# First block of a light convolution with a ReGLU layer: who fetches taps and x, and the order of the first convolution's matmuls

## The chip, the cores and the metric

The kernel runs on one core of a Trainium2 chip. The metric is the device time of one execution in microseconds (us), as the median of several runs. A core has TensorE (PE, matrix products into PSUM; its weight loads are listed apart as PEld), VectorE (DVE), ScalarE (ACT), GpSimd (POOL) and SyncE (SP). SP, ACT and POOL can issue DMA transfers. Each engine works through its own list of instructions in order and waits for the others by semaphores.

## The reference

Eight sequences x of 4096 tokens with 192 channels go through a causal convolution of 7 taps. The taps are a softmax over each of the 8 heads' 7 weights, and a head covers 24 channels. The result goes through a gated layer: 1536 gate columns with ReLU, times 1536 value columns, times an output matrix back to 192 channels.

```python
w = weight - np.max(weight, axis=-1, keepdims=True)
w = np.exp(w)
w = w / (np.sum(w, axis=-1, keepdims=True) + 1e-09)
x_pad = np.concatenate([np.zeros((B, pad, D), dtype=np.float32), x], axis=1)
x_unf = x_pad[:, idx, :].reshape(B, S, K, H, group)
out = np.einsum('hk,bskhg->bshg', w, x_unf)
...
gate = np.maximum(x @ w_gate, 0.0)
val = x @ w_val
return (gate * val @ w_out).astype(np.float32)
```

## The kernel before

Two sequences, called the streams (st), are worked on at a time, one on each half of the 128 partitions. A unit is 1024 tokens of both streams, and 16 units cover everything. The 192 channels are cut into three pieces of 64 (c), so a piece of both streams fills 128 partitions.

For most units the convolution is done off TensorE: x is turned by DMA transposes and multiplied with the taps on VectorE, ScalarE and GpSimd while TensorE does the gate, value and output products of the unit before. The first unit has no unit before it. Its convolution is done on TensorE, as products with band matrices, in two blocks of 512 tokens (`first_block` and `second_block`). The change lies in the first block and in what leads up to it.

What leads up to it, with the lines of the kernel before:

- SyncE fetches the 8 x 7 weights into `wr` (L110), then the body of stream 0's first 512 tokens in fp32 into the room `prods` (L131). GpSimd fetches the body of stream 1, cast to fp16, into `x_h` (L134), then the first 96 tokens of both streams (L135), then pieces of the gate and value matrices Wg and Wv (L170).
- VectorE sets `ones`, and ScalarE takes the Exp of it into `spare`, which nobody reads (L141 to L144). An Exp needs a table, and the load of the table stands right ahead of the first Exp on ScalarE's list.
- TensorE multiplies constants (`warm_up`, L154) while it has no data.
- The softmax: VectorE finds the maximum (L272), ScalarE takes the exponential (L275), VectorE sums, inverts and multiplies (L277 to L281).
- The bands: TensorE spreads the softmax over 112 rows (L289), VectorE puts it on diagonals (L299), 14 matmuls put the diagonals in their places (L309), and VectorE casts the bands to fp16 in four pieces (L336): heads 0 to 2, head 3, heads 4 and 5, heads 6 and 7.
- ScalarE casts stream 0's body from the room into `x_h` (L321), in two parts.

Then `conv_dense` makes the first block. The 512 tokens are cut into five steps (jj): the first 96 tokens are step 0, and four steps of 104 tokens follow. For each piece c it walks over the steps 1, 2, 3, 4, 0; in each over two halves (`second`, for the two heads that a run of 32 channels can touch), the two streams and two runs of 32 channels (k2). One such matmul has up to 32 output columns of the array, and `tile_position` (0, p0) with p0 = 64 st + 32 k2 says which of the four groups of 32 columns it uses. A piece needs 40 matmuls (five steps, two halves, two streams, two runs), the block 120. The pieces are finished one after the other, and each is copied out of PSUM into `xc` as soon as it is done: pieces 0 and 1 by ScalarE, piece 2 by VectorE (L388).

`gate_val` then makes the gate and value products (L550), 128 columns at a time. Its first tile takes the pieces in the order 0, 1, 2. Its second tile needs the copy of the next columns of Wg to the other partition half, which VectorE makes behind its copy of piece 2 (L177 from L805).

The kernel is scheduled by hand: the order of the statements is the order on each engine, and the tile framework adds the semaphore waits.

Of the kernel before, what the change touches and what calls it, by code (L numbers as in the profile page):

```python
# [8 lines left out]
FP = mybir.dt.float32  # L9
# [3 lines left out]
ACTF = mybir.ActivationFunctionType  # L13
# [4 lines left out]
def kernel(  # L18
# [12 lines left out]
    nc = tc.nc  # L31

    B, S, D = x.shape
    H, KW = weight.shape
# [29 lines left out]
    const = ctx.enter_context(tc.tile_pool(name="const", bufs=1))  # L64
# [9 lines left out]
    psum = ctx.enter_context(tc.tile_pool(name="psum", bufs=4, space=bass.MemoryType.PSUM))  # L74
# [32 lines left out]
    SEG = 16  # L107
    NSEG = SUB // SEG
    wr = const.tile([H, KW], FP)
    nc.sync.dma_start(out=wr[:], in_=weight)  # L110
    room = apool.tile([128, KW, NCH, LPOOL], FP, name="prods")

    def stage(p0, rows, st, n_st, jj, n):
        at = room[p0 : p0 + rows, 0, 0, 0:1]
        dims = [[D * GSUB, n_st], [D, n], [1, D]]
        return bass.AP(
            tensor=at.tensor,
            offset=at.offset + D * (GSUB * st + jj),
            ap=[at.ap[0]] + [d for d in dims if d[1] > 1],
        )  # L120
# [3 lines left out]
    def body(st):  # L124
# [7 lines left out]
    steps = const.tile([SUB, 64], I32)  # L132
# [3 lines left out]
        out=xts[0][PAD : PAD + FIRST, 0, :, :],  # L136
        in_=bass.AP(
            tensor=x.tensor, offset=x.offset, ap=[[D, FIRST], [NB * S * D, 2], [1, D]]
        ),
    )  # L140
    ones = const.tile([H, 1], FP)  # L141
    nc.vector.memset(ones[:], 1.0)
    spare = const.tile([H, 1], FP)
    nc.scalar.activation(spare[:], ones[:], ACTF.Exp)  # L144
    nc.vector.memset(xts[0][0:PAD, 0, :, :], 0.0)

    places = const.tile([SUB, 2 * SUB], F16)
# [27 lines left out]
    def both_halves(copy, s, dst):  # L175
        cols = slice(CUTS[s], CUTS[s + 1])
        copy(out=dst[64:128, :, cols], in_=dst[0:64, :, cols])  # L177
# [82 lines left out]
    with nc.allow_low_precision("zero and one"):  # L260
        nc.vector.tensor_tensor(
            out=same[:], in0=col[:, 0:SEG], in1=s_of[:].to_broadcast([SUB, SEG]), op=ALU.is_equal
        )
        nc.vector.tensor_scalar(
            out=places[:, SUB - SEG : SUB - SEG + NROW],
# [7 lines left out]
        out=mx[:], in_=wr[:], axis=mybir.AxisListType.X, op=ALU.max, negate=True  # L273
# [6 lines left out]
    with nc.allow_low_precision("rounded as the band is"):  # L280
        nc.vector.tensor_scalar(  # L281
            out=soft[:],
# [7 lines left out]
        out=spread[0:SUB, 0, 0:H],  # L290
# [7 lines left out]
    with nc.allow_low_precision("products with one and zero"):  # L298
        nc.vector.tensor_tensor(  # L299
            out=diag[:],  # L300
# [6 lines left out]
    for a in range(2):  # L307
        for b in range(NSEG):
            nc.tensor.matmul(  # L309
                out=(bps, spread)[a][:, a, HB * SEG * b : HB * SEG * (b + 1)],  # L310
# [9 lines left out]
    for cols in (slice(0, 64), slice(64, D)):  # L320
        nc.scalar.copy(  # L321
            out=xts[0][0:ROWS0, 1:GSUB, 0, cols],
            in_=stage(0, ROWS0, 0, 1, 1, GSUB - 1)[:, :, cols],
# [22 lines left out]
    def band(h):  # L346
        return bands[h]
# [2 lines left out]

    def conv_dense(g, c, ps, bank):


        xt = xts[g]
        toks = GROUPS[g][1]
        t0 = toks[0]
        ends = toks[1:] + [t0 + WIN]
        for jj in (1, 2, 3, 4, 0):  # L360
            col, n = toks[jj] - t0, ends[jj] - toks[jj]
            rows = n + PAD
            for second in range(2):
                for st in range(2):
                    for k2 in range(2):
                        k = 2 * c + k2
                        h0, h1 = 32 * k // G, (32 * k + 31) // G
                        h, m = (h0, G * h1 - 32 * k) if second else (h1, 32)
                        p0 = 64 * st + 32 * k2
                        nc.tensor.matmul(  # L370
                            out=ps[p0 : p0 + m, bank, col : col + n],
                            lhsT=xt[0:rows, jj, st, 32 * k : 32 * k + m],
                            rhs=band(h)[0:rows, 0:n],
                            start=True,
                            stop=True,
                            tile_position=(0, p0),
                            skip_group_check=True,
                        )

    def first_block():  # L380
        xc[0] = xcpool.tile([128, NCH, UNIT], F16, name="xc")
        both_halves(nc.vector.tensor_copy, 0, Wg)
        both_halves(nc.vector.tensor_copy, 0, Wv)
        for c in range(NCH):
            ps = psum.tile([128, 2, 512], FP, name="ps")
            conv_dense(0, c, ps, 0)
            copy = nc.vector.tensor_copy if c == 2 else nc.scalar.copy
            copy(out=xc[0][:, c, 0:WIN], in_=ps[:, 0, :])  # L388

    def second_block():  # L390
        two, one = [psum.tile([128, 2, 512], FP, name="ps") for _ in range(2)]
        conv_dense(1, 0, two, 0)
        conv_dense(1, 1, two, 1)
        nc.scalar.copy(out=xc[0][:, 0:2, WIN : 2 * WIN], in_=two[:])
        conv_dense(1, 2, one, 0)
        nc.vector.tensor_copy(out=xc[0][:, 2, WIN : 2 * WIN], in_=one[:, 0, :])
# [392 lines left out]


    first_block()
    taps = const.tile([H, KW], FP)
    nc.scalar.activation(taps[:], ex[:, 0:KW], ACTF.Copy, scale=sm[:])
    tap = const.tile([128, NCH, KW], FP)
    for h in range(H):
        r = G * h
        while r < G * (h + 1):
            c, n = r // 64, min(64 - r % 64, G * (h + 1) - r)
            nc.sync.dma_start(
                out=tap[r % 64 : r % 64 + n, c, :],  # L800
                in_=taps[h : h + 1, :].unsqueeze(1).to_broadcast([1, n, KW]),
# [98 lines left out]
```

## Time and profile before

| what | us |
|---|---|
| median of 3 runs | 762.16 |
| the runs | 761.86, 762.16, 766.11 |
| span of the profiled execution, first to last instruction | 759.9 |
| TensorE busy in it | 756.1 |
| VectorE busy | 707.4 |
| ScalarE busy | 617.3 |
| GpSimd busy | 404.9 |

The profile is of one execution. Its span covers the instructions; the runs' time has 2.26 us around it that no instruction shows. Times in rows are counted from the span's start. In the chain of waits each row is a start, a length and the work that the end was waiting for at that time. In the timeline a row is a start, a length, the engine, the line, the operation, out<-in with shapes, the count of merged instructions, and in brackets the idle time before it with what ended it.

### The profile page before, as it was taken

Reading aid. Unit: us, or ns where it says so; the run is one execution under the profiler, and the core shown is the slowest. Engines: PE = TensorE matmul, PEld = TensorE weight load, DVE = VectorE, ACT = ScalarE, POOL = GpSimd, SP = SyncE. Lnnn points to the kernel's source line nnn. Section 1 sums busy time; section 2 is a strip of 40 time slices with the busy share of each in tenths; the row PEclk is TensorE's granted clock in tenths of the full one; section 3 lists DMA queues with packets and bytes.
Section 4 is the critical chain, followed back from the end, with each engine's and each line's share of the span. In section 5 each row is a group of like instructions: output and inputs, shape, how many; then the busy total and the mean of one; then the engine's idle time right before and its main releaser. Section 6 shows DMA issues by size and latency. Waiting matters only on the chain.

```text
span 759.9 us, 30608 instructions
## 1 busy us (share of the span) xinstructions
PE 756.1 (99%) x13623; PEld 484.0 (64%) x13623; DVE 707.4 (93%) x768; ACT 617.3 (81%) x719; POOL 404.9 (53%) x263
## 2 busy tenths in 40 slices
PE   9999999999999999999999999999999999999998
PEld 5495555555666666666666666666666776666548
DVE  7998999999999999999999999999999999999891
ACT  6887887978879798897988879788798887976671
POOL 9519449094580936819276291863908548091000
PEclk9999999999999999999999999999999999999999
DMA  9969029688395894949759498594957939654732
GB/s 118 132 113 136 16 68 157 162 107 181 94 184 146 91 180 105 190 128 105 195 93 184 119 138 180 81 186 114 170 145 100 189 98 160 140 107 113 185 87 85
DMA packets 231308, 100.33 MB, mean 132 GB/s; under 512 B 185288, under 2 KB 220424, under 8 KB 231176
## 3 DMA queue, kind: packets, MB, share of 16 engines
q1 hardware_dynamic: 189928, 82.71, 53.1%
q0 software_dynamic: 41104, 15.57, 20.7%
q8 instruction: 106, 1.74, 1.0%
q14 instruction: 26, 0.21, 0.1%
q10 hardware_dynamic: 144, 0.10, 0.0%
HBM read 31.48 MB, written 47.19 MB: 104 GB/s over the span
## 4 chain that ended last, share of the span: by engine, by line
PE 99%; ACT 0%; issue 0%
PE ps L550 66%; PE ps L658 29%; PE ps L579 3%; PE ps L628 1%; PE ps L154 0%; PE ps L370 0%; PE ps L309 0%; PE ps L411 0%; ACT acc L605 0%; PE ps L289 0%
## 5 line engine op out<-in xcount | busy, mean ns | idle before, releaser
L562 DVE TENSOR_TENSOR hT<-gr,ps 128x1024 f16<-128x1024 f16 (+1 forms) x386 | 469.0, 1216 | 30.0 <-ACT gr L561 3.3
L561 ACT ACTIVATE gr<-ps 128x1024 f16<-128x1024 f32 (+1 forms) x386 | 393.3, 1020 | 100.7 <-PE ps L550 100.3
L498 POOL TENSOR_TENSOR prods<-prods 128x1344 f32<-128x1344 f32 x70 | 212.9, 3042 | 268.7 <-DVE prods L494 265.3
L550 PE MATMUL ps<-xc,Wg 64*64 64x512 f16 (+1 forms) x4320 | 321.9, 376 | 0.0
L550 PE MATMUL ps<-xc,Wv 64*64 64x512 f16 (+1 forms) x4320 | 321.6, 376 | 0.0
L658 PE MATMUL ps<-hT,Wo 64*64 64x512 f16 x4032 | 220.3, 376 | 0.0
L550 PEld LDWEIGHTS <-Wg 64*64 64x64 f16 (+1 forms) x4320 | 154.0, 106 | 94.9 <-issue 0.7
L550 PEld LDWEIGHTS <-Wv 64*64 64x64 f16 (+1 forms) x4320 | 152.7, 105 | 95.8 <-issue 0.3
L658 PEld LDWEIGHTS <-Wo 64*64 64x64 f16 x4032 | 140.2, 107 | 77.4
L522 DVE SCALAR_TENSOR_TENSOR acc<-x_r,tap,acc 128x576 f32<-128x576 f16 x225 | 165.3, 814 | 0.0
L492 ACT ACTIVATE prods<-x_r,tap 128x448 f32<-128x448 f16 x222 | 127.2, 659 | 0.0
L680 ACT COPY x_h<-ps 128x2048 uint16<-128x2048 uint16 x28 | 51.8, 1848 | 8.8 <-PE ps L658 8.8
L208 POOL DMA_DIRECT2D x_e<-in_x_dram x58 | 46.9, 818 | 12.3 <-ACT acc L508 12.0
L472 POOL COPY x_p<-x_e 128x960 f16<-128x960 f16 (+1 forms) x58 | 50.5, 912 | 0.5 <-DMA x_e<-in_x_dram 0.5
L498 POOL TENSOR_TENSOR xc<-prods 128x1344 f16<-128x1344 f32 x14 | 42.5, 3037 | 1.1
L680 POOL COPY y<-x_h 128x2048 uint16<-128x2048 uint16 x14 | 26.6, 1897 | 23.3 <-ACT x_h L736 23.3
L522 DVE SCALAR_TENSOR_TENSOR xc<-x_r,tap,acc 128x576 f16<-128x576 f16 x45 | 34.1, 813 | 0.0
L508 ACT ACTIVATE acc<-x_r,tap 128x576 f32<-128x576 f16 x45 | 31.4, 765 | 0.0
L494 DVE TENSOR_SCALAR prods<-x_r,tap 128x448 f32<-128x448 f16 x70 | 27.7, 448 | 0.0
L579 PE MATMUL ps<-Wo,hT 64*128 64x192 f16 x576 | 24.6, 243 | 0.0
L579 PEld LDWEIGHTS <-hT 64*128 64x128 f16 x576 | 23.9, 94 | 0.5
L736 ACT COPY x_h<-ps 128x512 f32<-128x512 f32 x14 | 8.2, 587 | 10.9 <-ACT x_h L680 5.5
(62 smaller groups left out, 91.6 us busy)
## 6 DMA issues: line engine op xcount, KB each, us to landing
out_dram<-out_s SPq DMA_DIRECT2D x62, 384.0 KB
held<-x_h SPq DMA_DIRECT2D x14, 512.0 KB
held<-x_h SPq DMA_DIRECT2D x28, 256.0 KB
held<-y SPq DMA_DIRECT2D x14, 512.0 KB
x_e<-in_x_dram POOLq DMA_DIRECT2D x34, 192.0 KB, 6.7
x_e<-in_x_dram POOLq DMA_DIRECT2D x24, 240.0 KB, 5.4
x_r<-x_p SPq DMA_TRANSPOSE x131
out_s<-held SPq DMA_TRANSPOSE x56
```

Source lines behind the costliest of these rows:

```text
L208: first = nc.gpsimd.dma_start(out=xe[:, j0 + start : j0 + n, st, :, :].rearrange("p j c r -> p j (c r)"), in_=bass.AP(tensor=x.tensor, off ...
L472: nc.gpsimd.tensor_copy(out=xp[:, j0 : j0 + n, :, st, :], in_=xe[:, j0 : j0 + n, st, :, :])
L492: engine.activation(out=out, in_=in_, func=ACTF.Copy, scale=scale)
L498: nc.gpsimd.tensor_tensor(out=pr[:, 0] if k < KW - 1 else xc[v + 1][:, :, LDVE:UNIT], in0=pr[:, 0], in1=pr[:, k], op=ALU.add,)
L508: nc.scalar.activation(out=accs[v][:, c, :], in_=shifted(v, c, 0, 0), func=ACTF.Copy, scale=tap[:, c, 0:1],)
L522: nc.vector.scalar_tensor_tensor(out=xc[v][:, c, 0:LDVE] if k == KW - 1 else acc[:, c, :], in0=shifted(v, c, k, 0), scalar=tap[:, c, k : k ...
L550: nc.tensor.matmul(out=pss[i][m : m + M, st, :], lhsT=W[64 * st : 64 * st + 64, c, 128 * f + m : 128 * f + m + M], rhs=xcb[64 * st : 64 * ...
L561: nc.scalar.activation(out=gr[:, sts], in_=pss[0][:, sts], func=ACTF.Relu)
L562: nc.vector.tensor_tensor(out=h[:, f, sts], in0=gr[:, sts], in1=pss[1][:, sts], op=ALU.mult)
L579: mm = nc.tensor.matmul(out=outs[q], lhsT=h[64 * r : 64 * r + 64, f, st, 128 * q : 128 * (q + 1)], rhs=Wo[64 * r : 64 * r + 64, f, :], sta ...
L658: mm = nc.tensor.matmul(out=ps[bank][64 * half : 64 * half + 64], lhsT=Wo[64 * r : 64 * r + 64, f, d : d + 64], rhs=hs[w][64 * r : 64 * r ...
L680: copy(out=pt[:], in_=src[:].bitcast(U16).rearrange("p b (t l) -> p b l t", l=2))
```

## The change

Three edits. ScalarE's queue issues the transfer of the weights into `wr`, so that SyncE's first transfer is x. The pair `ones` and `spare` is gone. In `first_block` the steps 1 to 4 of the pieces 0 and 1 go ahead, first all of stream 0, then all of stream 1; step 0 of these pieces follows, and then piece 2 in the old order. `conv_dense` takes the steps and the streams as arguments for it.

```diff
-    nc.sync.dma_start(out=wr[:], in_=weight)
+    nc.scalar.dma_start(out=wr[:], in_=weight)
...
-    ones = const.tile([H, 1], FP)
-    nc.vector.memset(ones[:], 1.0)
-    spare = const.tile([H, 1], FP)
-    nc.scalar.activation(spare[:], ones[:], ACTF.Exp)
...
-    def conv_dense(g, c, ps, bank):
+    def conv_dense(g, c, ps, bank, steps=(1, 2, 3, 4, 0), streams=(0, 1)):
...
-        for jj in (1, 2, 3, 4, 0):
+        for jj in steps:
...
-                for st in range(2):
+                for st in streams:
...
+        pss = [psum.tile([128, 2, 512], FP, name="ps") for _ in range(2)]
+        for st in range(2):
+            for c in range(2):
+                conv_dense(0, c, pss[c], 0, (1, 2, 3, 4), (st,))
         for c in range(NCH):
-            ps = psum.tile([128, 2, 512], FP, name="ps")
-            conv_dense(0, c, ps, 0)
+            if c == 2:
+                pss.append(psum.tile([128, 2, 512], FP, name="ps"))
+            ps = pss[c]
+            conv_dense(0, c, ps, 0, (1, 2, 3, 4, 0) if c == 2 else (0,))
             copy = nc.vector.tensor_copy if c == 2 else nc.scalar.copy
             copy(out=xc[0][:, c, 0:WIN], in_=ps[:, 0, :])
```

How the instructions stand on an engine, with what each waits for, is shown at two places. The first is the start of ScalarE's list, before. DMAHW0 is the transfer of the weights, DMAHW1 the transfer of x by SyncE.

```order
L144 ACT_TABLE_LOAD
L144 ACTIVATE spare<-ones 8x1 [waits DVE_49]
L275 ACTIVATE ex<-wr,mx 8x7 [waits DMAHW0_49,DVE_49]
L321 CAST x_h<-prods 110x4x64 [waits DMAHW1_49]
L321 CAST x_h<-prods 110x4x128
```

The same place now:

```order
L110 DMA wr<-in_weight_dram 8x7
L271 ACT_TABLE_LOAD [waits DMAHW0_49]
L271 ACTIVATE ex<-wr,mx 8x7 [waits DVE_49]
L317 CAST x_h<-prods 110x4x64 [waits DMAHW1_49]
L317 CAST x_h<-prods 110x4x128
```

The table load stood first and waited for nothing. Now it stands behind the issue of the weights' transfer, ahead of the real exponential, and the wait for that transfer stands on the load.

The second place is the start of the first convolution on TensorE, before. band_182 is the tile with the bands of heads 0 to 2, and DMASW0 is GpSimd's transfer of stream 1's body.

```order
L370 LDWEIGHTS x_h [waits Activation_49]
L370 MATMUL ps<-band_182,x_h 32x104 [waits DVE_49]
L370 LDWEIGHTS x_h
L370 MATMUL ps<-band_182,x_h 32x104
L370 LDWEIGHTS x_h [waits DMASW0_49]
L370 MATMUL ps<-band_182,x_h 32x104
```

The same place now, where band_178 is that same tile of heads 0 to 2:

```order
L366 LDWEIGHTS x_h [waits Activation_49]
L366 MATMUL ps<-band_178,x_h 32x104 [waits DVE_49]
L366 LDWEIGHTS x_h
L366 MATMUL ps<-band_178,x_h 32x104
L366 LDWEIGHTS x_h
L366 MATMUL ps<-band_178,x_h 24x104
L366 LDWEIGHTS x_h
L366 MATMUL ps<-band_178,x_h 16x104
```

Before, stream 1 was needed by the third matmul, and four matmuls of a kind in a row went to the four column groups. Now two of a kind go to the two groups of stream 0, then two of the next kind to the same two groups, and stream 1 is first waited for ahead of the 33rd matmul.

## The prediction

> **What bounds the kernel now.** I read the page's head first, then the chain of waits in order of time, then the timeline of the first 16 us, and last single groups and transfers in that stretch.
>
> The page's head says how much room there is at all.
>
> ```profile
> span 759.9 us, 30608 instructions
> PE 756.1 (99%) x13623; PEld 484.0 (64%) x13623; DVE 707.4 (93%) x768; ACT 617.3 (81%) x719; POOL 404.9 (53%) x263
> ```
>
> TensorE is busy for 756.1 of 759.9 us. An edit can only matter by making TensorE wait, by giving it more to do, or by changing the speed at which it does it. The chain (start, length, what) shows where the edited code lies in it.
>
> ```profile
> 0.78 2.72 PE ps L154 x6
> 3.50 0.18 PE ps L289
> 3.68 0.54 PE ps L154
> 4.22 0.75 PE ps L309 x14
> 4.96 0.32 PE ps L154
> 5.28 1.95 PE ps L370 x117
> 7.23 6.74 PE ps L550 x60
> 13.97 1.62 PE ps L370 x113
> 15.59 24.71 PE ps L550 x228
> ...
> 756.88 0.02 issue
> 756.90 0.32 ACT acc L605
> ```
>
> The change touches only what lies before the first gate matmul (L550, 7.23). From 15.59 to the end the chain is matmuls without a gap, so whatever the first gate tiles lose or gain is handed to the end one for one. What the start waits for is in the timeline (start, length, engine, line, in brackets the idle time before it and who ended it):
>
> ```profile
> 0.73 1.28 ACT L144 ACT_TABLE_LOAD   x1 [0.73 <-PEq L884]
> 0.74 0.40 SPq L110 DMA_DIRECT2D wr<-in_weight_dram  x1
> 1.20 0.34 SPq L131 DMA_DIRECT2D prods<-in_x_dram  x1
> 1.41 0.89 POOL L134 DMA_DIRECT2D x_h<-in_x_dram  x1 [0.40 <-issue]
> 2.03 0.20 ACT L144 ACTIVATE spare<-ones 8x1 f32<-8x1 f32 x1
> 2.11 0.15 DVE L272 TENSOR_REDUCE mx<-wr 8x1 f32<-8x7 f32 x1 [0.30 <-DMA wr<-in_weight_dram]
> 2.29 0.30 ACT L275 ACTIVATE ex<-wr,mx 8x7 f32<-8x7 f32 x1
> 2.30 0.69 POOL L135 DMA_DIRECT2D x_h<-in_x_dram  x1
> 3.42 0.16 PEld L289 LDWEIGHTS <-soft 8*112 8x112 f16 x1 [0.84 <-DVE soft L281]
> 3.71 0.29 DVE L299 TENSOR_TENSOR diag<-ps,same 112x128 f16<-112x128 f32 x1 [0.40 <-PE ps L289]
> 4.63 1.28 DVE L336 CAST band<-ps 128x336 f16<-128x336 f32 x4 [0.62 <-PE ps L309]
> 4.65 0.93 ACT L321 CAST x_h<-prods 110x256 f16<-110x256 f32 x2 [2.06 <-DMA prods<-in_x_dram]
> 5.21 2.02 PE L370 MATMUL ps<-band,x_h 110*32 110x104 f16 x120
> 6.34 1.08 ACT L388 CAST xc<-ps 128x512 f16<-128x512 f32 x2 [0.76 <-PE ps L370]
> 7.17 0.39 PE L550 MATMUL ps<-xc,Wg 64*128 64x512 f16 x2
> 7.28 0.69 DVE L388 CAST xc<-ps 128x512 f16<-128x512 f32 x1 [0.37 <-PE ps L370]
> 8.00 0.56 DVE L177 COPY Wg<-Wg 64x768 f16<-64x768 f16 x1
> 8.62 0.33 PEld L550 LDWEIGHTS <-Wg 64*128 64x128 f16 x5 [0.27 <-DVE Wg L177]
> ```
>
> Two chains meet at 5.21. One is the band: taps landed (2.11), exponential (2.29), softmax, spread matmul (3.42), diagonal (3.71), 14 matmuls, band in fp16 (4.63). The other is x: landed and cast by ScalarE (4.65). The groups by form and the transfers (KB, us from issue to landing) show how close they are.
>
> ```profile
> L336 DVE CAST band<-ps 128x336 f16<-128x336 f32 x1 | 0.5, 509 | 0.6 <-PE ps L309 0.6
> L321 ACT CAST x_h<-prods 110x256 f16<-110x256 f32 x1 | 0.4, 405 | 2.1 <-DMA prods<-in_x_dram 2.1
> x_h<-in_x_dram POOLq DMA_DIRECT2D x1, 168.0 KB, 3.8
> x_h<-in_x_dram POOLq DMA_DIRECT2D x1, 72.0 KB, 3.7
> ```
>
> The first band is ready at 4.63 + 0.51 = 5.14, the first cast of x at 4.65 + 0.41 = 5.06, the second stream's body at 1.41 + 3.8 = 5.2, the first rows at 2.30 + 3.7 = 6.0. Three conditions end within 0.15 us of each other, so moving only one of them earlier is worth about 0.1 us. Moving one later costs all of it.
>
> **The table load loses its cover.** The removed pair (ones, and the Exp of ones into spare) did no arithmetic that anybody reads, but ScalarE's table load stood in front of it and waited for nothing: 0.73 to 2.01, beside the flight of the taps, which the reduction sees landed at 2.11. In the changed program the load stands in front of the real exponential and waits for the taps' transfer, as the order of ScalarE shows. It starts at about 2.11, ends at 2.11 + 1.28 = 3.39, and the exponential follows at 3.41 where it stood at 2.29: **+1.12 us** on the band's chain, with nothing beside it. Queued behind the load on ScalarE are the exponential and the two casts of x. The exponential would end at 3.71, x has not landed by then, and the casts lose nothing. Behind the exponential wait VectorE's sum, TensorE's spread and every step down to 5.21, which becomes 6.33.
>
> The trace does not show a taps transfer issued by ScalarE beside x. At best it lands as now (SyncE issued it at 0.74, and ScalarE is free at 0.73). At worst it shares the engines with x and loses what x's issue took beside it, about 0.4 us. I take 0, since the transfer is 0.2 KB, and keep 0.4 for the range.
>
> **x first on SyncE.** x is issued at 0.74 instead of 1.20, so by estimate it lands 0.46 us earlier and the first cast is done near 4.6. The band is ready only at 5.14 + 1.12 = 6.26. Worth **0**. If the load did not wait, it would be worth the 0.1 above.
>
> **The order by streams.** One stream's matmuls fill two of the four 32-column groups (p0 is 64 st + 32 k2). The 64 moved matmuls (two channel pieces, four steps, two halves, two k2, two streams) therefore go in 32 rounds of two where they went in 16 rounds of four. A round lasts as long as one group needs for 104 columns. At full speed the gate matmuls, which fill two groups of 64 rows, give 24.71/228 = 0.108 us each, so 0.217 us for 512 columns in a group: 44 ns for 104. The second block's 120 in 1.62 (13.97) give at most 56 ns for a round of four. I take 50 ns, so 16 more rounds cost **+0.8 us** at full speed. At the start speed the warm-up of 384 columns took 0.32 us (4.96): 87 ns, and 16 rounds are **+1.4 us**. What the order was to hide, the arrivals at 5.2 and 6.0, is over at 6.33 anyway.
>
> It has a second price. Channel piece 0 was complete after 40 matmuls and ScalarE copied it at 6.34, while TensorE was still convolving. Now pieces 0 and 1 are complete only 16 matmuls after the 64, and just piece 2 (40 matmuls) is left to hide two copies of 0.54 us.
>
> **The speed of TensorE.** Its weight loads in the first convolution, in two windows (count: min/median/max ns, first and last start):
>
> ```profile
> L370 PEld LDWEIGHTS <-x_h x24: 90/137/147, 5.2 to 5.6; 110*32 110x32 f16 x12, 110*24 110x24 f16 x6, 110*16 110x16 f16 x6
> L370 PEld LDWEIGHTS <-x_h x88: 82/93/97, 6.0 to 7.0; 110*32 110x32 f16 x32, 110*8 110x8 f16 x16, 102*32 102x32 f16 x12, 110*24 110x24 f16 x8
> ```
>
> TensorE turned to full speed between 5.6 and 6.0, say 5.8, about 5.0 us after its first matmul, and it had worked nearly without a gap since 0.78. In the changed kernel the warm-ups end at 3.50 as now, but the spread comes at 3.42 + 1.12 = 4.54: a hole of 1.0 us that the trace of before does not have. From below the hole costs nothing (full speed still at 5.8). From above the count of 5.0 us begins again at 4.7, when the warm-up behind the spread starts, and full speed comes at 9.7. I take the upper end, since in this trace full speed came only after an unbroken stretch.
>
> The Trainium skill, "TensorE: Matmul & The Clock Gate", section "What's actually happening", says that the clock doubles after a free-running window of about 3.4 us was busy, sustained. The trace agrees with it: 5.0 us lies between one window and two. For the changed kernel the page puts full speed between 8.1 and 11.5, and by my reckoning the time would be an estimated 764.4 to 765.7 us.
>
> **The sum**, on the profile's clock. Convolution from 6.33. One stream at a time, at half speed: 32 x 0.087 = 2.78, to 9.11. First rows of pieces 0 and 1: 4 rounds, 0.34, to 9.45. Piece 2: 3 rounds to 9.7, then 7 x 0.05, to 10.06, and about 0.2 us for the last matmul's own length: 10.26, against 7.23 now. From there to the second gate tile the path is VectorE's, copy of piece 2 and then the copy of Wg: 8.62 - 7.23 = 1.39. So the second gate tile starts at 11.65 instead of 8.62, **+3.0**. The path over ScalarE ends earlier: piece 0 done at 9.28, copied about 0.25 later in 0.54, first gate matmul near 10.2, twelve of 0.108 us, 11.5. From 8.62 to 13.97 stand 48 matmuls, 5.2 us of work in 5.35, so up to 0.15 of small waits can be absorbed; I take 0.1. **Net +2.9 us**: the span goes from 759.9 to 762.8. The median of the runs, 762.16, lies 2.26 us above the span, so the time is 762.16 + 2.9 = **765.1 us** (0.4% more).
>
> **Rivals.**
>
> *Full speed is not delayed (0.36).* The hole is short and the matmuls around it suffice. Then 32 x 0.05 = 1.6 to 7.93, first rows to 8.13, piece 2 to 8.63, end 8.83, second gate tile by VectorE at 10.22. By ScalarE: copy of piece 0 from 8.28 to 8.82, of piece 1 to 9.36, first tile done at about 10.3. That is +1.7, less 0.1: **763.8**. For it: the hole is 1.0 us of 5.8. Against it: the unbroken stretch that the trace needed.
>
> *The load doesn't wait after all (0.05).* If ScalarE starts the load on its own while the taps fly, the convolution starts at 5.21 and full speed comes at 5.8. Seven rounds at half speed, 25 at full, first rows to 7.27, end near 8.0, first tile by ScalarE at about 9.46: +0.8, less 0.1, **762.9**. Against it stands the wait written on the load.
>
> *Not slower (0.04).* The same, and the rounds of two cost no more than rounds of four, because the weight loads and not the columns set the pace. Then 120 matmuls take the second block's 1.62 instead of 1.95, as arrivals no longer hold them, and **761.8** results. It decides if the load starts before about 1.0, so that it ends before the reduction at 2.26. The two-group rate above speaks against the second half.
>
> *The load costs more than its row (0.05).* If the load cannot be followed at once and takes its own length again, 1.28 us more fall on the chain: **766.4**. In the trace the activation started at 2.03, right behind the load's end at 2.01, which speaks against it. The Trainium skill, "ScalarE: Activation LUTs", section "What ACT_TABLE_LOAD costs", gives 1283 ns and a drain of about 1380 ns on top. The trace agrees with the first number and shows no drain, and the measurement decides.
>
> **Chances and range.** Forecast 0.50, full speed in time 0.36, and 0.14 for the others, as given. The range takes in the first two: from 763.8 less 0.6 (full-speed rounds of 44 ns instead of 50, and the 0.3 between the two lower runs, 761.86 and 762.16) = 763.2, to 765.1 plus 0.4 for late taps and 0.6 for half speed to the end of the first tile = 766.1. What falls outside is 0.14. One per cent is 7.6 us, about what a measurement of this kernel can tell from no change, and no case reaches half of that: the same 0.97. Faster by over 1% 0.01, slower by over 1% 0.02, for a mechanism that I don't see.
>
> **What would show it.** In the profile of the changed kernel: the table load begins at about 2.1, not 0.7, and ends right before the exponential (step one). VectorE's first band cast starts near 5.75 and the convolution near 6.3. The line of the first convolution takes over 3 us for 120 matmuls if half speed holds, about 2.5 if not, and weight loads of 130 to 147 ns last past 9 us or stop near 6. ScalarE's wait for x ends before the convolution's inputs are needed. The first gate matmul stands near 10.2. From the second block on, all rows are those of before, shifted by one constant. I am wrong if the load begins before 1, if the 64 matmuls run as fast as rounds of four, or if the stages after the second block change their lengths, which nothing in the diff touches.

## The result and the profile after

The changed kernel takes 764.44 us (median of 22 runs, 763.05 to 766.27), the kernel before 762.40 us in the same jobs (22 runs). The ratio is 1.0025 with a 95% interval of 1.0018 to 1.0031: slower by 2.0 us in the medians, or by 0.25% in the ratio. Forecast were 765.1 us and a range of 763.2 to 766.1. The ratio is not the quotient of the two medians, which is 1.0027; in these runs the two differ by a tenth of a per cent at most.

In every run on record the time lies 1.7 to 1.9 us above the run's own span (here 764.37 and 762.6 in the profiled execution). The 2.26 us named ahead of the prediction compare the median of three runs with the span of one fast execution, so some 0.5 us of them is a difference between executions. The forecast does not hang on it, but differences of spans to that profile come out larger than differences of medians.

The page's head of the changed kernel:

```profile
span 762.6 us, 30606 instructions
PE 757.4 (99%) x13623; PEld 483.0 (63%) x13623; DVE 707.6 (93%) x767; ACT 616.7 (81%) x718; POOL 404.9 (53%) x263
```

The span grew by 2.7 us and TensorE's busy time by 1.3. So TensorE both worked longer on the same 13,623 matmuls and waited longer. The chain of waits shows where.

```profile
0.74 1.36 DMA wr<-in_weight_dram
...
2.17 1.28 ACT L271
...
3.47 0.31 ACT ex L271
...
4.54 0.22 PE ps L285
...
5.53 0.52 DVE band L332
...
6.09 3.38 PE ps L366 x105
9.47 7.01 PE ps L552 x60
16.48 1.48 PE ps L366 x117
17.96 24.73 PE ps L552 x228
```

Before, the chain was TensorE's own from 0.78 on. Now it begins with the taps' transfer and runs through the table load, the exponential, the spread and the first band. From 6.09 on it is TensorE's, but for a stretch near 338 us that the last experiment takes up. The first convolution fills 3.38 us of the chain instead of 1.95. The same stretch in the timeline:

```profile
0.74 0.59 ACTq L110 DMA_DIRECT2D wr<-in_weight_dram  x1
2.12 0.15 DVE L268 TENSOR_REDUCE mx<-wr 8x1 f32<-8x7 f32 x1 [0.34 <-DMA wr<-in_weight_dram]
2.17 1.28 ACT L271 ACT_TABLE_LOAD   x1 [2.17 <-DMA wr<-in_weight_dram]
3.47 0.30 ACT L271 ACTIVATE ex<-wr,mx 8x7 f32<-8x7 f32 x1
3.99 0.92 ACT L317 CAST x_h<-prods 110x256 f16<-110x256 f32 x2 [0.23 <-DMA prods<-in_x_dram]
4.54 0.21 PE L285 MATMUL ps<-same,soft 8*112 8x8 f16 x1 [1.04 <-DVE soft L277]
5.13 0.57 PE L305 MATMUL ps<-diag,places 112*128 112x64 f16 x14
6.09 3.38 PE L366 MATMUL ps<-band,x_h 110*32 110x104 f16 x120 [0.23 <-DVE band L332]
8.50 1.07 ACT L390 CAST xc<-ps 128x512 f16<-128x512 f32 x2 [3.59 <-PE ps L366]
9.41 0.61 PE L552 MATMUL ps<-xc,Wg 64*128 64x512 f16 x2
11.11 0.81 PE L552 MATMUL ps<-xc,Wg 64*128 64x512 f16 x6
```

The exponential starts 1.18 us later than before (3.47 against 2.29). TensorE stands idle for 1.04 us ahead of the spread. The second gate tile starts at 11.11. Its row before was this one:

```profile
8.47 0.97 PE L550 MATMUL ps<-xc,Wg 64*128 64x512 f16 x6
```

So it starts 2.6 us later. The 8.62 that the prediction took for it is the load of its second weights, which waited 0.27 us for the copy of Wg; now none of its loads waits for that copy. In the chain what follows the second block, the 228 gate and value matmuls, stands at 17.96 instead of 15.59, 2.4 us later.

Busy times by window show what the hole did to the clock. The columns are the window, its length, the busy us of each engine (PE, PEld, DVE, ACT, POOL) with its instruction count, the granted clock, the DMA engines' busy share and GB/s. The clock column knows the clock only from its first change on; ahead of it it reads 1.00, though the start runs at half speed (six matmuls of 512 columns took 2.72 us there, 0.45 each, where the prediction reads 0.217 at full speed).

```profile
0.00:3.40 3.40, 2.62 (x6) 0.73 (x6) 1.10 (x10) 1.23 (x1) 2.36 (x8) 1.00 0.38 100
3.40:6.80 3.40, 2.07 (x48) 1.46 (x50) 2.18 (x8) 1.28 (x4) 3.40 (x7) 1.00 1.12 118
6.80:10.20 3.40, 3.40 (x105) 2.73 (x101) 1.37 (x4) 1.25 (x3) 2.75 (x4) 0.51 1.17 128
```

In this execution full speed came early (the 14 placement matmuls took 0.57 us, before 0.91). In the window from 3.4 to 6.8 TensorE was busy for only 2.07 us, and in the next one it ran at 0.51 of its clock. The convolution's weight loads say the same, early and late:

```profile
L366 PEld LDWEIGHTS <-x_h x23: 83/94/98, 6.1 to 6.7; 110*32 110x32 f16 x12, 110*24 110x24 f16 x5, 110*16 110x16 f16 x3, 110*8 110x8 f16 x3
L366 PEld LDWEIGHTS <-x_h x74: 81/128/148, 7.2 to 9.1; 110*32 110x32 f16 x24, 110*8 110x8 f16 x12, 102*32 102x32 f16 x12, 110*16 110x16 f16 x9
```

### The profile page after: what moved, and what is told of

Its sections match the earlier page's. It is cut to its first block, busy times and chain, and to the rows that moved or that the text cites. A ratio compares the mean times of both kernels' runs of the same rounds, so it can differ in the third digit from the quotient of the medians.

```text
span 762.6 us, 30606 instructions
## 1 busy us (share of the span) xinstructions
PE 757.4 (99%) x13623; PEld 483.0 (63%) x13623; DVE 707.6 (93%) x767; ACT 616.7 (81%) x718; POOL 404.9 (53%) x263
## 4 chain that ended last, share of the span: by engine, by line
PE 98%; DVE 1%; ACT 0%; DMA 0%; issue 0%; ACTq 0%
PE ps L552 65%; PE ps L660 28%; PE ps L581 3%; PE ps L630 1%; PE ps L366 1%; DVE prods L496 0%; DMA wr<-in_weight_dram 0%; ACT L271 0%; DVE hT L564 0%; DVE xc L524 0%; DVE x_h L739 0%; PE ps L413 0%; DVE band L332 0%; PE ps L305 0%; DVE soft L277 0%
```

## The experiments

Each was timed beside the kernel before. "First gate" is the start of the first gate matmul in the profiled execution; it was 7.17 before and 9.41 after.

| run | median us | before, same job | ratio, 95% interval | first gate |
|---|---|---|---|---|
| e1_load_early | 762.96 | 762.29 | 0.9997, 0.9974 to 1.0019 | 7.77 |
| e2_no_spare | 764.06 | 762.29 | 1.0019, 1.0010 to 1.0028 | 7.58 |
| e3_streams | 762.18 | 762.29 | 1.0000, 0.9991 to 1.0009 | 7.90 |
| e4_queue | 763.68 | 762.29 | 1.0015, 1.0005 to 1.0024 | 9.08 |
| e5_fill | 763.53 | 762.23 | 1.0013, 0.9995 to 1.0031 | 9.36 |
| e6_x_first | 764.32 | 762.23 | 1.0034, 1.0021 to 1.0046 | 9.22 |
| e7_hole | 763.07 | 762.23 | 1.0012, 1.0003 to 1.0021 | 8.04 |
| e8_no_spare_fill | 763.09 | 762.23 | 1.0009, 0.9992 to 1.0026 | 7.85 |
| e9_ones | 764.18 | 762.15 | 1.0025, 1.0016 to 1.0034 | 9.46 |

### The three edits apart

e1_load_early is the changed kernel with the pair put back:

```diff
+    ones = const.tile([H, 1], FP)
+    nc.vector.memset(ones[:], 1.0)
+    spare = const.tile([H, 1], FP)
+    nc.scalar.activation(spare[:], ones[:], ACTF.Exp)
```

> The changed kernel with the pair ones and spare put back: the table load stands ahead of everything on ScalarE again, the queues and the order by streams stay as changed. Load theory (the load's wait for the taps is most of the loss): the convolution starts near 5.2 again and the time falls from about +2.0 us over the kernel before to +0.5 to +0.9, what the order by streams costs by itself. Order theory (rounds of two are most of the loss): the time stays at +1.5 or more. Speed theory (the hole in TensorE's early work decides by way of half speed): the hole from 3.50 to 4.54 is gone, and the time falls to within 0.3 us of the kernel before.

The median fell from 764.44 to 762.96, to 0.67 above the kernel before. That fits the load theory; the ratio puts it 0.2 us below the kernel before, and its interval (about 1.7 us each way) does not part the load theory from the speed theory. The order theory asked for +1.5 and is the worst fit. The rows of its start (timeline):

```profile
0.74 0.59 ACTq L110 DMA_DIRECT2D wr<-in_weight_dram  x1
1.36 1.28 ACT L144 ACT_TABLE_LOAD   x1 [1.36 <-PEq L890]
2.77 0.28 ACT L275 ACTIVATE ex<-wr,mx 8x7 f32<-8x7 f32 x1
5.43 2.20 PE L370 MATMUL ps<-band,x_h 110*32 110x104 f16 x120 [0.23 <-DVE band L336]
```

The issue of the taps' transfer holds ScalarE for 0.59 us, and the table load stands behind it. The load now ends after the taps have landed, and the exponential starts at 2.77 instead of 2.29. No step of the prediction priced that.

e2_no_spare is the kernel before without the pair:

```diff
-    ones = const.tile([H, 1], FP)
-    nc.vector.memset(ones[:], 1.0)
-    spare = const.tile([H, 1], FP)
-    nc.scalar.activation(spare[:], ones[:], ACTF.Exp)
```

> The kernel before without the pair ones and spare, nothing else changed. Load theory: the load starts at about 2.1, the convolution starts 0.9 to 1.2 us later than 5.21, and the time rises by 0.8 (full speed in the convolution) to 1.9 us (half speed). Order theory: less than 0.5 us. Speed theory: between the two, by the phase of the turn to full speed; in the profile either a stretch of half speed after the hole, with +1.5 or more, or none, with +0.8.

The median rose by 1.77 us; the ratio puts it at 1.45 us (0.8 to 2.1). The load alone reaches most of the whole change, and the order theory's limit of 0.5 is excluded. In the profile:

```profile
2.16 1.28 ACT L271 ACT_TABLE_LOAD   x1 [2.16 <-DMA wr<-in_weight_dram]
3.45 0.30 ACT L271 ACTIVATE ex<-wr,mx 8x7 f32<-8x7 f32 x1
6.08 1.57 PE L366 MATMUL ps<-band,x_h 110*32 110x104 f16 x120 [0.23 <-DVE band L332]
7.58 0.39 PE L546 MATMUL ps<-xc,Wg 64*128 64x512 f16 x2
```

The load waits for the taps with the old queues too. This execution happened to run the whole convolution at full speed (120 matmuls in 1.57 us), so its first gate matmul is only 0.4 us late, while the median is late by 1.8. (Its span of 768.1 is not used: a transfer of x landed late near 30 us, and the gate matmuls behind it start 7.3 us later than before, at 64.12 instead of 56.82.)

e3_streams has the order by streams alone: the taps back on SyncE, ones and spare kept, `first_block` as changed.

```diff
+                conv_dense(0, c, pss[c], 0, (1, 2, 3, 4), (st,))
...
+            conv_dense(0, c, ps, 0, (1, 2, 3, 4, 0) if c == 2 else (0,))
```

> The kernel before with the order by streams alone (taps and x on SyncE as before, ones and spare kept). Order theory: +1.5 us or more. Load theory: +0.5 to +0.9 us, for rounds of two and for the copies of pieces 0 and 1 that come late. If weight loads set the pace of the convolution and not the columns: 0, and the 64 matmuls take as long as 64 in rounds of four.

The time is that of the kernel before (1.0000, 0.7 us each way). The order theory is out. The 0.5 to 0.9 of the load theory lies at the edge of the interval. The matmuls do take longer in rounds of two: at full speed 2.20 us for 120 in e1 and in e5, against 1.57 in e2 and in e8, 0.63 us for 16 more rounds.

e4_queue is the kernel before with the taps on ScalarE's queue:

```diff
-    nc.sync.dma_start(out=wr[:], in_=weight)
+    nc.scalar.dma_start(out=wr[:], in_=weight)
```

> The kernel before with the taps fetched by ScalarE's queue alone. All theories: x is issued 0.46 us earlier and lands about that much earlier, but the band (5.14) and the second stream (5.2) hold the convolution, so between -0.15 and +0.1 us. If taps land later beside x: up to +0.4 us, and the reduction over the taps starts after 2.3.

The ratio means +1.1 us (0.4 to 1.8), the median +1.4. The taps landed as ever (reduction at 2.11), so neither sentence of the expectation holds. The rows that bear on it:

```profile
1.36 1.28 ACT L144 ACT_TABLE_LOAD   x1 [1.36 <-PEq L884]
4.26 0.92 ACT L321 CAST x_h<-prods 110x256 f16<-110x256 f32 x2 [1.22 <-DMA prods<-in_x_dram]
5.61 0.27 PE L370 MATMUL ps<-band,x_h 110*32 110x104 f16 x2
6.40 2.75 PE L370 MATMUL ps<-band,x_h 110*32 110x104 f16 x118 [0.52 <-DMA x_h<-in_x_dram]
```

Beside the late table load, the body of stream 1 is late: the third matmul needs it and waits until 6.40, where it had landed at 5.2 before. From issue to landing it took 4.9 us here, 4.6 in the changed kernel, 4.5 in e1, 5.0 in e5, 4.8 in e6 and 4.7 in e9, all with x first; with the taps first it took 3.8 (before, e2, e7), 4.1 (e8) and, once, 4.7 (e3). GpSimd issued it at the same time in all. So an early x seems to push it back, by 0.7 to 1.2 us in most executions, and in these profiles the order by streams keeps it off the convolution's start (in e1, with the same transfers, the 120 matmuls run from 5.43 without a stop; e4 stops until 6.40).

The clock has a part in this profile too. It is the slowest of e4's eleven executions (765.18 us), and by the clock records of the traces it came to full speed at 12.6 us, the profile of the kernel before at 5.8: the 118 matmuls took 2.75 us. How much of the 1.1 us is the late table load, how much the late stream 1 and how much the clock, no run parts.

### x ahead of the taps on one queue

e6_x_first is the kernel before with SyncE's first two transfers exchanged:

```diff
-    nc.sync.dma_start(out=wr[:], in_=weight)
...
     nc.sync.dma_start(out=stage(0, SUB, 0, 1, 1, GSUB - 1), in_=body(0))
+    nc.sync.dma_start(out=wr[:], in_=weight)
```

> The kernel before with SyncE's first two transfers exchanged, x ahead of the taps; ones, spare and the order of the convolution as before, ScalarE issues nothing. It splits what the queue change alone cost (+1.4 us in the median). If the loss came from the early x (GpSimd's body of stream 1 lands later when x goes ahead): stream 1's body lands more than 4.4 us after its issue and the convolution waits for it until 6 or later, +0.7 to +1.5 us. If it came from ScalarE's issue of the taps, 0.58 us ahead of the table load: the load starts at 0.74 again; what is left is the taps' issue 0.4 us later, which holds the band back by about as much, +0.3 to +0.5 us, and stream 1 lands within 4 us of its issue.

Stream 1 lands late (4.8 us after issue), as the first reading asked. But something else, expected by neither, is larger:

```profile
1.19 0.42 SPq L131 DMA_DIRECT2D wr<-in_weight_dram  x1
4.19 0.15 DVE L272 TENSOR_REDUCE mx<-wr 8x1 f32<-8x7 f32 x1 [2.37 <-DMA wr<-in_weight_dram]
4.37 0.30 ACT L275 ACTIVATE ex<-wr,mx 8x7 f32<-8x7 f32 x1 [2.14 <-DVE mx L272]
6.99 2.29 PE L370 MATMUL ps<-band,x_h 110*32 110x104 f16 x120 [0.23 <-DVE band L336]
```

The taps' 0.2 KB, issued behind x on the same queue, land 3.0 us after their issue, about when an x that goes first lands (its cast starts at 3.99 to 4.26 in the changed kernel, e1, e4 and e9). The run doesn't separate stream 1's lateness from that, since the band came later than both. A part of its loss is the clock: TensorE stood idle for 1.95 us ahead of the spread, and full speed, granted by 4.2, was gone from 7.6 to 11.0.

### The hole and the clock

Three runs vary only warm-up matmuls. e5_fill adds three to the changed kernel, e8_no_spare_fill adds three to e2, and e7_hole takes three away from the kernel before:

```diff
-    warm_up(512, 512, 512, 512, 512, 512)
+    warm_up(512, 512, 512, 512, 512, 512, 512, 512, 512)
...
-    warm_up(512, 512, 512, 512, 512, 512)
+    warm_up(512, 512, 512)
```

> The changed kernel with three more warm-up matmuls of 512 columns behind the first six, so that TensorE works until about 4.6 at half speed and the hole from 3.50 to 4.54 is filled; nothing else differs. Speed theory (the hole makes the clock fall back, and half speed in the first convolution is a part of the loss): the time falls by 0.5 to 1.2 us against the changed kernel's 764.4, to 763.2 to 763.9, and the profile grants full speed by 4 to 8 us without a fall after it. Pure latency theory (the table load's 0.9 to 1.1 us of delay and the rounds of two are the whole loss): within 0.3 us of 764.4, or later by the 0.1 that the fill may hold up the spread.

> The kernel before without ones and spare (that alone gave +1.8 us in the median, a ratio of 1.0019) and with three more warm-ups that fill the hole before the spread. Speed theory: the time falls by 0.5 us or more against the same kernel without the fill (764.06), to 763.6 or less; what is left, +0.4 to +1.2 us, is the load's own delay. Latency theory: within 0.3 us of 764.06.

> The kernel before with three instead of six warm-up matmuls at the start: a hole in TensorE's work from about 2.2 to 3.4, and no data comes later. Speed theory: full speed is granted later in many executions, up to 3.4 us later, and the time rises by 0.4 to 1.5 us. Latency theory: within 0.3 us of the kernel before, since nothing waits for warm-ups.

All three medians went the way of the speed theory. Filling the hole took 0.9 us off the changed kernel (764.44 to 763.53) and 1.0 us off e2 (764.06 to 763.09); with each median set against the kernel before of its own job it is 0.7 and 0.9. Making a hole where no data is late cost 0.8 us (ratio 1.0012, 1.0003 to 1.0021). The weight loads of the first convolution, in e5, e8 and e7 in turn:

```profile
L366 PEld LDWEIGHTS <-x_h x120: 82/93/97, 6.7 to 9.0; 110*32 110x32 f16 x48, 110*24 110x24 f16 x16, 110*16 110x16 f16 x16, 110*8 110x8 f16 x16
```

```profile
L366 PEld LDWEIGHTS <-x_h x120: 83/93/97, 6.0 to 7.7; 110*32 110x32 f16 x48, 110*24 110x24 f16 x16, 110*16 110x16 f16 x16, 110*8 110x8 f16 x16
```

```profile
L370 PEld LDWEIGHTS <-x_h x120: 85/138/147, 5.2 to 7.7; 110*32 110x32 f16 x48, 110*24 110x24 f16 x16, 110*16 110x16 f16 x16, 110*8 110x8 f16 x16
```

In e5 and e8 all of them run at full speed; in e7 none does, and its clock record has full speed from 8.9 on, that of the kernel before from 5.8. But e5's hole was not filled in this execution. Its table load started at 3.09, held until then by the taps' transfer, which landed 0.9 us later than in the changed kernel's own profile, with the same queues, and so TensorE stood idle behind the nine warm-ups:

```profile
5.46 0.21 PE L285 MATMUL ps<-same,soft 8*112 8x8 f16 x1 [0.84 <-DVE soft L277]
```

So e5's profile, like e2's, shows a hole that cost no speed. The intervals of the first two are 1.3 us wide each way and overlap those of the kernels without the fill, so the size of each step is a matter of medians; their agreement and e7's interval carry the conclusion.

Why one execution loses the speed and another doesn't shows when the windows are laid on the moments at which the clock turned. In the changed kernel they are 3.42, 6.83 and 10.25, and in every trace the turns lie a whole number of steps of 3.41 us apart, with a start of the steps that differs by execution. The same windows in e2, e6 and e9, which have the six first warm-ups of the changed kernel (here PE alone, then clock, DMA share and GB/s; in e2 full speed came at 4.20 and stayed, in e9 it first came at 8.31):

```profile
4.20:7.61 3.41, 2.79 (x139) 1.00 1.33 136
```

```profile
4.19:7.60 3.41, 1.87 (x70) 1.00 1.24 141
7.60:11.01 3.41, 3.41 (x94) 0.50 1.16 135
```

```profile
1.49:4.90 3.41, 2.38 (x7) 1.00 0.79 136
4.90:8.31 3.41, 3.41 (x72) 1.00 1.28 145
```

In e2 most of the hole lies ahead of 4.20, and the speed stays. In the changed kernel and in e6 the hole lies in a window at full speed that holds only 2.07 and 1.87 us of work, and the next window runs at half speed. In e9 it lies in a window ahead of the first turn, which then comes one window later. So in these profiles the hole costs speed by where the steps fall on it. In e5 the window from 4.33 to 7.74 held 2.28 us, and the speed stayed. One trace does not fit a bound on busy time alone: e4 stayed at half speed behind windows with 3.09 and 2.90 us of work.

### A small loss far from the edit

e9_ones is the changed kernel with the memset alone:

```diff
+    ones = const.tile([H, 1], FP)
+    nc.vector.memset(ones[:], 1.0)
```

> The changed kernel with only the memset of ones put back on VectorE (nobody reads it; no Exp of it, so the table load still waits for the taps). It is about a small loss far from the edit: near 338 to 341 us the chain of waits leaves TensorE for VectorE in the four profiles without the pair, and in none of the six with it, and costs about 0.35 us there. If the place of VectorE's instructions in its list decides (one instruction fewer than before), the chain stays on TensorE there again and the time falls by about 0.3 us against 764.4. If the missing Exp or the late start decides, the excursion to VectorE stays and so does the time. Either way the table load starts after 2.1 and the first part of the loss stays.

VectorE in the changed kernel near 338 us (timeline), and below it in e9:

```profile
338.25 0.81 DVE L496 TENSOR_SCALAR prods<-x_r,tap 128x448 f32<-128x448 f16 x2
339.51 0.69 DVE L739 COPY x_h<-ps 128x512 f32<-128x512 f32 x1 [0.45 <-issue]
```

```profile
337.98 0.82 DVE L498 TENSOR_SCALAR prods<-x_r,tap 128x448 f32<-128x448 f16 x2
338.89 0.69 DVE L741 COPY x_h<-ps 128x512 f32<-128x512 f32 x1
```

With the memset back, the pause of 0.45 us ahead of the copy is gone, and the chain stays on TensorE there. The pause stood in the four profiles with 767 VectorE instructions, and in none of the seven with 768. The median is 0.26 us lower than the changed kernel's, but against the kernel before of its own job the loss is the same 2.0 us, so the expected gain of 0.3 is not shown. Whether the pause is there follows VectorE's list; why it pauses was not tried.

No run is shown to beat the kernel before: e3 equals it.

## Why the prediction was right, point by point

- **The table load**: right in place and size. Start 2.17 (2.11 forecast), exponential 3.47 (3.41). e2 and e1 show it from both sides: taking the pair away alone costs 1.77 in the median, putting it back gains 1.48 (1.37 against the kernels before of the same jobs).
- **The taps on ScalarE's queue**: I took 0 with 0.4 as the bound. Four of the five profiles with this queue show no delay (the reduction starts at 2.11 or 2.12), e5's shows 0.9. The bound was too small. That the issue itself holds ScalarE for 0.59 us was missing; in the changed kernel it is hidden, because the load waits for the taps until 2.17 anyway.
- **x first**: worth 0, as forecast. It landed earlier (the cast starts at 3.99 instead of 4.65), and the band was the last to come. What I left out is that stream 1's body lands later for it.
- **Rounds of two**: 0.8 us forecast at full speed, 0.63 measured. The 1.4 for half speed has no run of its own.
- **The speed**: the right mechanism, but its form differs by execution. The prediction had full speed come for the first time at 9.7, because "in this trace full speed came only after an unbroken stretch". In the changed kernel's profile it was granted at 3.4 already, taken away at 6.8 for one window of 3.4 us, and given back. In e9's, where TensorE does the same work, it came for the first time at 8.3, so there the forecast form holds. That the changed kernel's own profile still ran the convolution mostly at half speed is luck as far as the forecast goes: the hole happened to lie in one window.
- **The sum**: several steps were off and in part made up for each other. The convolution started at 6.09 (6.33 forecast), since the 14 placement matmuls ran at full speed, and ended at 9.47 (10.26). From there the forecast path to the second gate tile was VectorE's copies, 1.39 us; in the profile the tile waits for no copy and stands behind the first tile's own matmuls, 1.64 us. It came out at +2.6 (+3.0 forecast), the span at +2.7 (+2.9). Of the span's growth 0.3 is the stretch near 338 us, a stage behind the second block that changed its length: by the prediction's own list a sign of being wrong, and not foreseen.
- **The time**: 764.4 lies between the forecast (765.1) and the rival with full speed (763.8). Counted as a rise over the kernel before, the measured 2.0 us is nearer to the rival (1.6) than to the forecast (2.9). The term that was mis-sized is the price of half speed: I charged 1.3 us in every execution, the difference of these two cases. The fill showed 0.7 to 0.9 in the medians. e2's profile, in which the same hole cost no speed at all, shows why: executions differ in this by where the clock's steps fall on the hole, so the forecast and its rival are, as far as these profiles tell, two kinds of execution of one kernel, and the median lies between them.
- **The other rivals**: the load did wait, which ends the two with a free load. The one with 1.28 us more is out as well: the exponential follows the load within 0.02 us. The drain on top of the load that the Trainium skill gives ("ScalarE: Activation LUTs", section "What ACT_TABLE_LOAD costs") is not seen here.

## What to carry to other kernels

An instruction that computes nothing may hold the place of something that does: here a dead Exp pulled a table load of 1.28 us to where it waited for nothing, and without it the load took over the wait of the next Exp. Read from the instruction order where such a wait ends up before you take out "dead" code. A hole of 1 us in TensorE's early work can cost nearly as much again by way of the clock (0.7 to 0.9 us in the medians here), in some executions and not in others. Filler matmuls gained that back here, though in e8 they held the spread up by 0.2 us (4.71 against e2's 4.53).

## What the runs showed of the hardware

- The clock went back to half after windows of 3.4 us in which TensorE had been busy for 2.07 us (the changed kernel) and 1.87 us (e6), so not only after an idle one; it stayed full after 2.28 us (e5) and 2.79 us (e2). The Trainium skill ("TensorE: Matmul & The Clock Gate", section "What's actually happening") has the clock go cold after an idle window of about that length; the rows of the changed kernel and e6 decide otherwise.
- A small transfer behind a large one on one queue landed 3.0 us after its issue (e6), against 1.4 us ahead of it (0.74 to 2.1, before).
- The issue of a transfer by ScalarE took 0.59 us of that engine ahead of its table load (e1, e4).
- VectorE paused for 0.45 us, without a wait that the profile shows, ahead of one copy near 338 us in the profiles with 767 instructions on its list, and not in those with 768 (e9 among them).
